# First chunk of a decaying-state attention kernel: the tables zeroed by ScalarE, the ones filled behind the power table, own-key columns from that table, and other due times

## The chip, the cores and the metric

The kernel runs on one core of a Trainium2 chip. The metric is the device time of one execution in microseconds (us), the median over several. Engines are named as the profile names them: PE (matmul, with PEld for its weight loads), DVE (VectorE), ACT (ScalarE), POOL (GpSimd), SP (SyncE, which here only issues transfers).

## The reference

Two parts follow one another. The first is attention with a state that decays, for 4 batches, 8 heads, 768 times and 48 channels; the second is an MLP on its output:

```
for t in range(S):
    cur = einsum('bhd,bhe->bhde', u[None] * k_t, v_t)
    y[:, :, t] = einsum('bhd,bhde->bhe', r_t, state + cur)
    state = w[None, :, :, None] * state + einsum('bhd,bhe->bhde', k_t, v_t)
x = y as [B*S, H*D] = [3072, 384]
out = gelu(x @ w_in) @ w_out          # w_in [384, 2048], w_out [2048, 384]
```

## The kernel before

**Chunks and groups.** The 768 times are cut into 6 chunks of 128; a chunk of all 4 batches is 512 columns for the MLP. The 8 heads go in pairs, so each chunk has 4 groups. Inside a chunk the recurrence is written as products: r and k of a group are scaled by powers of the decay w, their product gives the scores, past scores are kept by a mask, and the scores times v are the output. The own-time term (u) is a sum of r times k, weighted.

**The MLP.** A chunk takes 16 steps. Each has 9 products of 512 columns into `Hp` (L667: x times w_in, in high and low parts), gelu twice on ACT (`gh`, L696, and `gf`, L697), the low part on DVE (`gl`, L698), and 9 products into `O` (L709). The weights come in 64-bit words and are split into `wh` and `wl` during the first chunk, a weight pair for each step, by four ACT and three DVE operations (L382 to L395).

**The order.** Each operation is entered with `add(engine, ns, due, function, r=reads, w=writes)`. `Plan.run` walks a model of the engines with these assumed durations and issues what is ready, by due time; an operation that is entered with `LATER` takes its due time from those that need it. That fixes each engine's order. The names in `r` and `w` set only the planned order: waits on the chip come from the tiles that an instruction really reads and writes. Where the plan sees PE idle it fills in matmuls on zeros (`heat`, L283).

**The first chunk.** SP issues the loads one behind the other: `wu_sb` (w and u), then `T` and `N` of group 0, of group 1, and so on, with the first weights from the seventh on. Meanwhile:

- POOL fills `ones`, makes the masks `diag`, `past` and `ident` of it (L250), and zeroes `Fm` (L265) and `VO` (L266) twice each, `UB` (L330), `E` (L341) and `Am` (L268, twice).
- DVE zeroes `zeros` (the operand of `heat`), and makes the power table `F` from w: it limits w to its range (L303), doubles the powers (L297), and multiplies by a reciprocal. Then it makes `E1`, whose transpose gives `WN`.
- A group scales `T` by `F` (L555), multiplies its halves into `KB` (L559; POOL, for group 0 DVE), and has `N` scaled by `WN` on POOL (L561). PE makes the scores (L568, into `A` or `AE`) and the own sums (L573: `KB` times the columns of `UB`, into `UE`). DVE puts the past scores into `Fm` (L599) and the own sums times v into `VO` (L602). PE multiplies `VO` and `Fm` into `Y` (L588, L594); groups 1 to 3 first add columns of group 0 (`gaps`, L583). ACT and DVE take `Y` as the high and low part of x (L534, L535: `x3` for group 0, `xx` for the others). First sums for the state (L578) are copied to `Sa` (L612), which frees the PSUM banks that `Hp` and `O` take over.
- `UB` holds w times u for each pair: `uw` is made on DVE (L319, L320) and copied into place on POOL (L325).

Of the kernel before, what the change touches and what calls it, by code (L numbers as in the profile page):

```python
# [9 lines left out]
F32 = mybir.dt.float32  # L10
# [5 lines left out]
ALU = mybir.AluOpType  # L16
# [5 lines left out]
C = 128  # L22
# [3 lines left out]
NB = B  # L26
TOK = NB * C
NJ = DF // 128
HALF = 64
# [8 lines left out]
LATER = 10 ** 7  # L38
# [8 lines left out]
class Plan:  # L47
# [11 lines left out]
    def add(self, eng, ns, at, fn, r=(), w=()):  # L59
        n = len(self.ops)  # L60
        deps = set()
        for x in r:
            deps.add(self.writer.get(x))
            self.readers.setdefault(x, []).append(n)
        for x in w:
            deps.add(self.writer.get(x))
            deps.update(self.readers.pop(x, ()))
            self.writer[x] = n
        deps -= {None, n}
        self.ops.append((eng, ns, at, fn, deps))  # L70
        self.reads.append(set(r))
# [66 lines left out]
def rwkv_gelu_mlp(tc, rkT, rkv, wuT, uN, wmlp, r, k, vT, w, u, out):  # L138
    nc = tc.nc
    with ExitStack() as ctx:  # L140
# [21 lines left out]
        w_sb = wu_sb[:, 0:2 * NP]  # L162
        u_lane = wu_sb[:, 2 * NP:]
# [8 lines left out]
        E = sb([LP, NP, 2, HALF], F32, "E")  # L172
        F = sb([LP, NP, C], F32, "F", pro)
# [3 lines left out]
        UB = sb([LP, NP, 2], F32, "UB", pro)  # L177
        Fm = [sb([C, 2, NB, C], F32, f"Fm{i}", pro) for i in range(2)]
        VO = [sb([C, NB, 2, 64], F32, f"VO{i}", pro) for i in range(2)]
        uw = sb([LP, 2 * NP], F32, "uw")  # L180
# [4 lines left out]
        Am = [sb([C, 2, NB, HALF], F32, f"Am{i}") for i in range(2)]  # L185
# [11 lines left out]
        zeros = sb([128, 512], F32R, "zeros", pro)  # L197
# [4 lines left out]
        add, dma = plan.add, plan.dma  # L202
        dve = lambda n: 65 + n / 0.96
        dve2 = lambda n: 65 + n / 1.92
        act = lambda n: 95 + n / 1.2
        sdve = lambda n: 145 + n / 0.96
        sdve2 = lambda n: 145 + n / 1.92
        sact = lambda n: 250 + n / 1.2
        pool = lambda n: 110 + n * 2.15
# [35 lines left out]


        add("pool", 140, 0, lambda: nc.gpsimd.memset(ones, 1.0), w=["ones"])

        def masked(dst, base, cm, op):
            nc.gpsimd.affine_select(out=dst, in_=ones, pattern=[[1, C]], base=base, channel_multiplier=cm,  # L250
# [5 lines left out]
        for dst, src, x in ((diag2, diag, "diag"), (past2, past, "past")):  # L256
            for h in range(2):
                add("act", 280, LATER, lambda dst=dst, src=src, h=h: nc.scalar.copy(
                    out=dst[64 * h:64 * h + 64], in_=src[64 * h:64 * h + 64, 64 - 64 * h:128 - 64 * h]),
                    r=[x], w=[f"{x}2{h}"])  # L260
        add("dve", 80, -10 ** 6, lambda: nc.vector.memset(warm, 0.0), w=["warm"])
        add("act", 1400, -10 ** 6, lambda: nc.scalar.activation(out=warm, in_=warm, func=AF.Gelu), w=["warm"])
        add("dve", 480, -20, lambda: nc.vector.memset(zeros.bitcast(F32), 0.0), w=["zeros"])
        for i in range(2):
            add("pool", 1100, 10 + i, lambda i=i: nc.gpsimd.memset(Fm[i], 0.0), w=[f"Fm{i}"])  # L265
            add("pool", 560, 20 + i, lambda i=i: nc.gpsimd.memset(VO[i], 0.0), w=[f"VO{i}"])  # L266
        for i in range(2):
            add("pool", 560, LATER, lambda i=i: nc.gpsimd.memset(Am[i], 0.0), w=[f"Am{i}"])  # L268


        def spread_ones():
# [22 lines left out]
        one = lambda x, i: x[:, :, i:i + 1]  # L294
# [4 lines left out]
        by_half = lambda x: x.rearrange("l (p h) -> l p h", h=2)  # L299
# [22 lines left out]
        def own_columns():  # L322
            for x in range(2):
                l = slice(64 * x, 64 * x + D)
                nc.gpsimd.tensor_copy(out=UB[l, :, x:x + 1], in_=by_half(uw)[l, :, 0:1])  # L325

        add("dve", 2150, 5, powers, r=["w_sb"], w=["F"])
        add("dve", 800, LATER, state_powers, r=["F"], w=["E1"])
        add("dve", 330, LATER, own_weights, r=["w_sb"], w=["uw"])
        add("pool", 110, LATER, lambda: nc.gpsimd.memset(UB, 0.0), w=["UB"])  # L330
        add("pool", 300, LATER, own_columns, r=["uw"], w=["UB"])


        def flip():
# [3 lines left out]
        add("pe", 700, LATER, flip, r=["E1", "ident"], w=["O1"])  # L338
        add("act", 500, LATER, lambda: nc.scalar.copy(
            out=WN, in_=AE[:, 1].rearrange("s (p j x) -> s p j x", p=NP, x=64)[:, :, :, :D]), r=["O1"], w=["WN"])  # L340
        add("pool", 560, LATER, lambda: nc.gpsimd.memset(E, 0.0), w=["E0"])  # L341


        def for_halves():
# [201 lines left out]
        def first_group(gi):  # L546
            g = Group(gi)
            i = gi % 2
            at = lambda ns: 4000 + 4300 * gi + ns
# [2 lines left out]
            fm, FM = Fm[i], f"Fm{i}"  # L552
            vo, VN = VO[i], f"VO{i}"
            flat = g.t.rearrange("l a b t -> l (a b) t")
            add("dve", sdve(1024), at(0), lambda: nc.vector.tensor_tensor(  # L555
                out=flat, in0=flat, in1=F[:, g.p].unsqueeze(1).to_broadcast([LP, 2 * NB, C]), op=ALU.mult),
                r=["F"], w=[g.T])
            eng, ns = (nc.gpsimd, 1300) if gi else (nc.vector, sdve(512))
            add("pool" if gi else "dve", ns, at(100), lambda: eng.tensor_tensor(  # L559
                out=own, in0=g.t[:, 1], in1=g.t[:, 0, :, ::-1], op=ALU.mult), r=[g.T], w=OWN)  # L560
            add("pool", pool(DM), LATER, lambda: nc.gpsimd.tensor_tensor(  # L561
                out=g.kn, in0=g.kn, in1=WN[:, g.p].rearrange("s j d -> s (j d)").unsqueeze(1).to_broadcast(
                    [C, NB, 2 * D]), op=ALU.mult), r=["WN"], w=[g.K])
# [27 lines left out]
            def first_new():  # L591
# [8 lines left out]
                out=fm, mask=past.bitcast(U32).unsqueeze(1).unsqueeze(1).to_broadcast([C, 2, NB, C]),  # L600
                data=g.x.rearrange("s x (b t) -> s x b t", t=C)), r=["past"] + g.X, w=[FM])
            add("dve", sdve(DM), at(3300), lambda: nc.vector.tensor_tensor(  # L602
                out=vo[:, :, :, :D], in0=g.vn.rearrange("s b (j d) -> s b j d", d=D),
                in1=sums.rearrange("s (b j) -> s b j", j=2).unsqueeze(3).to_broadcast([C, NB, 2, D]), op=ALU.mult),
                r=[SU, g.V], w=[VN])
            if spreads(g):
# [6 lines left out]
                out=g.s[2].rearrange("l b e -> l (b e)"), in_=g.u[:LP, g.u0:g.u0 + NB * D]), r=g.U, w=g.S[2])  # L613
# [242 lines left out]
        for G in range(NSTEP + 1):  # L856
# [12 lines left out]
            if G % 4 == 0 and G // 4 + NP < NG:  # L869
                gi = G // 4 + NP + 1  # L870
# [110 lines left out]
```

## Time and profile before

| what | us |
|---|---|
| median of 3 runs | 495.92 (495.48 to 496.24) |
| the profiled execution, its own time | 494.16 |
| its span on the core | 492.7 |
| PE busy | 480.5 (98%) |
| DVE busy | 227.9 (46%) |
| ACT busy | 219.0 (44%) |
| POOL busy | 76.9 (16%) |

The shares are means over stages. In the first 37 us PE works in small products that wait for others; from then on it runs the MLP nearly without a gap. Times in the rows below are counted from the start of the span.

### The profile page before, as it was taken

How to read it: one execution, taken by the hardware profiler on the slowest of the kernel's cores; microseconds unless marked ns; L12 is line 12 of the kernel's file. 1: busy time of each engine (PE TensorE's matmuls, PEld its weight loads, DVE VectorE, ACT ScalarE, POOL GpSimd, SP SyncE). 2: the span in 40 equal slices, each digit the busy share in tenths (PEclk: the TensorE clock that was granted, in tenths of full speed). 3: DMA queues.
4: the chain of work that ended last, by engine and by line, in shares of the span. 5: the costliest groups of instructions: out<-in, count | busy, mean ns of one | idle time of the engine just before them, and what ended most of it. 6: DMA issues, size and time to landing. Idle time of an engine off the chain costs nothing.

```text
span 492.7 us, 10760 instructions
## 1 busy us (share of the span) xinstructions
PE 480.5 (98%) x4684; PEld 389.0 (79%) x4684; DVE 227.9 (46%) x348; ACT 219.0 (44%) x449; POOL 76.9 (16%) x79
## 2 busy tenths in 40 slices
PE   6989999999999999999999999999999999999996
PEld 5877877878888878788888888888888887888885
DVE  7678889895525426414435434344344132211112
ACT  2179999976343343523342542442533423322222
POOL 6620100113012023302022021021120200000000
PEclk8799999999999999999999999999999999999999
DMA  8943666721403304303203313123223000100001
GB/s 242 354 117 122 237 205 208 225 56 53 142 2 97 97 2 130 118 0 97 72 27 97 113 39 98 37 60 98 79 72 97 1 14 12 65 1 0 1 0 67
DMA packets 13331, 43.79 MB, mean 89 GB/s; under 512 B 1824, under 2 KB 2208, under 8 KB 13280
## 3 DMA queue, kind: packets, MB, share of 16 engines
q1 hardware_dynamic: 13280, 43.07, 27.9%
q8 instruction: 37, 0.61, 0.5%
q14 instruction: 14, 0.11, 0.1%
HBM read 36.38 MB, written 4.72 MB: 83 GB/s over the span
## 4 chain that ended last, share of the span: by engine, by line
PE 90%; ACT 4%; DVE 4%; POOL 1%; issue 0%; DMA 0%; DVEq 0%; POOLq 0%
PE Hp L667 39%; PE O L709 38%; PE Y L480 2%; PE A L460 2%; PE Y L500 2%; PE Y L709 1%; PE A L471 1%; ACT wb L386 1%; DVE T L555 1%; PE Y L588 1%; DVE F L303 1%; PE Y L594 1%; POOL N L561 1%; ACT wb L388 1%; ACT wh L394 1%; ACT gf L697 1%
## 5 line engine op out<-in xcount | busy, mean ns | idle before, releaser
L667 PE MATMUL Hp<-xx,wh 128*128 128x512 f32 x576 | 166.7, 397 | 1.9 <-ACT gf L697 1.2
L698 DVE TENSOR_TENSOR gl<-gf,gh 128x512 fp32r<-128x512 f32 x95 | 68.9, 725 | 191.2 <-ACT gf L697 191.0
L696 ACT ACTIVATE gh<-Hp 128x512 fp32r<-128x512 f32 x95 | 56.7, 597 | 215.6 <-PE Hp L667 215.6
L667 PEld LDWEIGHTS Hp<-xx,wh 128*128 128x128 f32 x576 | 106.5, 188 | 28.3 <-ACT gf L697 3.3
L667 PE MATMUL Hp<-xx,wl 128*128 128x512 f32 x288 | 83.7, 398 | 0.9 <-DVE wl L395 0.9
L709 PE MATMUL O<-gh,wh 128*128 128x512 f32 (+1 forms) x285 | 82.0, 394 | 0.0
L709 PE MATMUL O<-gl,wh 128*128 128x512 f32 (+1 forms) x285 | 80.6, 390 | 0.0
L709 PE MATMUL O<-gh,wl 128*128 128x512 f32 (+1 forms) x285 | 80.6, 390 | 0.0
L667 PEld LDWEIGHTS Hp<-xx,wl 128*128 128x128 f32 x288 | 53.9, 188 | 14.4 <-DVE wl L395 1.7
L709 PEld LDWEIGHTS O<-gh,wh 128*128 128x128 f32 x285 | 52.5, 188 | 12.6
L709 PEld LDWEIGHTS O<-gl,wh 128*128 128x128 f32 x285 | 52.6, 188 | 11.7
L709 PEld LDWEIGHTS O<-gh,wl 128*128 128x128 f32 x285 | 52.5, 188 | 11.5
L431 POOL TENSOR_TENSOR Nb<-Nb 128x384 f32<-128x384 f32 x16 | 19.6, 1226 | 250.1 <-DMA Nb<-in_rkv_dram 220.0
L697 ACT ACTIVATE gf<-Hp 128x512 f32<-128x512 f32 x96 | 56.9, 593 | 0.0
L451 ACT ACTIVATE Am<-diag,cs 128x64 f32<-128x64 f32 x128 | 33.6, 341 | 10.1 <-DVE cs L446 9.5
L433 POOL TENSOR_TENSOR Nb<-Nb,WN 128x384 f32<-128x384 f32 x20 | 24.1, 1208 | 47.0 <-DMA Nb<-in_rkv_dram 44.4
L427 DVE TENSOR_TENSOR Tb<-Tb,E 112x1024 f32<-112x1024 f32 x20 | 24.4, 1221 | 4.7 <-DMA Tb<-in_rkT_dram 4.5
L446 DVE TENSOR_REDUCE cs<-Nb 128x8 f32<-128x384 f32 x16 | 8.8, 553 | 34.4 <-POOL Nb L443 34.3
L386 ACT ACTIVATE wb<-raw 128x768 uint16<-128x768 uint32 (+1 forms) x17 | 17.6, 1036 | 0.0
L388 ACT ACTIVATE wb<-raw 128x768 f16<-128x768 f32 (+1 forms) x17 | 17.6, 1034 | 0.0
L392 DVE CUSTOM_DVE_ANT_0 wa<-wa,wb 128x1536 uint16<-128x1536 uint16 (+1 forms) x17 | 16.3, 957 | 2.5 <-ACT wb L388 2.1
L443 POOL TENSOR_TENSOR Nb<-Nb,u_sb 128x384 f32<-128x384 f32 x16 | 17.0, 1064 | 0.1
(126 smaller groups left out, 400.1 us busy)
## 6 DMA issues: line engine op xcount, KB each, us to landing
raw<-in_wmlp_dram SPq DMA_DIRECT2D x15, 768.0 KB, 4.3
Nb<-in_rkv_dram SPq DMA_DIRECT2D x16, 576.0 KB, 5.4
Tb<-in_rkT_dram SPq DMA_DIRECT2D x20, 448.0 KB, 4.3
out_dram<-raw SPq DMA_DIRECT2D x5, 768.0 KB, 3.6
xx<-x SPq DMA_DIRECT2D x30, 64.0 KB, 4.2
T<-in_rkT_dram SPq DMA_DIRECT2D x4, 448.0 KB, 6.9
N<-in_rkv_dram SPq DMA_DIRECT2D x4, 384.0 KB, 7.4
Nb<-in_rkv_dram SPq DMA_DIRECT2D x4, 384.0 KB, 8.4
```

What stands on the lines that cost most here:

```text
L386: add("act", sact(n), LATER, lambda: nc.scalar.activation(out=parts[:, :, 0], in_=lo.bitcast(U32), func=AF.Copy, scale=2.0 ** -29), r=R_, ...
L388: add("act", sact(n), LATER, lambda: nc.scalar.activation(out=parts[:, :, 1].bitcast(F16), in_=hi.bitcast(F32), func=AF.Copy, scale=2.0 ** ...
L427: add("dve", sdve(1024), LATER, lambda: nc.vector.tensor_tensor(out=flat, in0=flat, in1=E[:, g.p].rearrange("l h i -> l (h i)").unsqueeze( ...
L431: add("pool", pool(DM), LATER, lambda: nc.gpsimd.tensor_tensor(out=g.n[:, 0], in0=g.n[:, 0], in1=g.n[:, 1], op=ALU.mult), r=[g.K], w=[g.R])
L433: add("pool", pool(DM), LATER, lambda: nc.gpsimd.tensor_tensor(out=g.kn, in0=g.kn, in1=WN[:, g.p].rearrange("s j d -> s (j d)").unsqueeze( ...
L443: add("pool", pool(DM), LATER, lambda: nc.gpsimd.tensor_tensor(out=g.n[:, 0], in0=g.n[:, 0], in1=u_sb[:, g.p, :].unsqueeze(1).to_broadcast ...
L451: add("act", sact(HALF) + 60, LATER, lambda x=x, b=b: nc.scalar.activation(out=g.am[:, x, b, :], in_=diag2, func=AF.Copy, scale=g.sums[:, ...
L667: nc.tensor.matmul(O[3], lhsT=wt[j][:, 0, k_ * 128:(k_ + 1) * 128], rhs=x[:, a, k_, :], start=start and k_ == ks[0], stop=stop and k_ == k ...
L696: add("act", 600, LATER, lambda: nc.scalar.activation(out=high, in_=O[3], func=AF.Gelu), r=["H"], w=[GH])
L697: add("act", 600, LATER, lambda: nc.scalar.activation(out=gf, in_=O[3], func=AF.Gelu), r=["H"], w=["gf"])
L698: add("dve", sdve(512), LATER, lambda: nc.vector.tensor_tensor(out=low, in0=gf, in1=high.bitcast(F32), op=ALU.subtract), r=["gf", GH], w=[GL])
L709: nc.tensor.matmul(bank(dst)[:, a:b], lhsT=wt[j][:, 1, d * 128:(d + 1) * 128], rhs=gt[:, a:b], start=(j == 0 and n == 0), stop=(j == NJ - ...
```

## The change

ScalarE zeroes `Fm` and `VO` by copying from `zeros`; the zeroing of `E` and `Am` is entered with `r=["F"]`; `UB` is computed by DVE from the table and u in place of the copies from `uw`; the plan is told 2900 ns for the table where it was told 2150; and scaling `T` of groups 1 to 3 is due 2500 ns sooner. Behind these edits the planner puts all engines' work of the first chunk in a new order.

```diff
         add("pool", 140, 0, lambda: nc.gpsimd.memset(ones, 1.0), w=["ones"])
+        add("dve", 480, -20, lambda: nc.vector.memset(zeros.bitcast(F32), 0.0), w=["zeros"])
...
-        add("dve", 480, -20, lambda: nc.vector.memset(zeros.bitcast(F32), 0.0), w=["zeros"])
         for i in range(2):
-            add("pool", 1100, 10 + i, lambda i=i: nc.gpsimd.memset(Fm[i], 0.0), w=[f"Fm{i}"])
-            add("pool", 560, 20 + i, lambda i=i: nc.gpsimd.memset(VO[i], 0.0), w=[f"VO{i}"])
-        for i in range(2):
-            add("pool", 560, LATER, lambda i=i: nc.gpsimd.memset(Am[i], 0.0), w=[f"Am{i}"])
+            add("act", 560, 20 + i, lambda i=i: nc.scalar.copy(
+                out=VO[i].rearrange("s b j d -> s (b j d)"), in_=zeros.bitcast(F32)), r=["zeros"], w=[f"VO{i}"])
+            add("act", 1050, 10 + i, lambda i=i: nc.scalar.copy(
+                out=Fm[i].rearrange("s j b t -> s j (b t)"),
+                in_=zeros.bitcast(F32).unsqueeze(1).to_broadcast([C, 2, NB * C])), r=["zeros"], w=[f"Fm{i}"])
...
-                nc.gpsimd.tensor_copy(out=UB[l, :, x:x + 1], in_=by_half(uw)[l, :, 0:1])
-
-        add("dve", 2150, 5, powers, r=["w_sb"], w=["F"])
+                nc.vector.tensor_tensor(out=UB[l, :, x:x + 1], in0=one(F, HALF + 1)[l], in1=by_half(u_lane)[l, :, 0:1],
+                                        op=ALU.mult)
+
+        add("dve", 2900, 5, powers, r=["w_sb"], w=["F"])
+        for i in range(2):
+            add("pool", 560, LATER, lambda i=i: nc.gpsimd.memset(Am[i], 0.0), r=["F"], w=[f"Am{i}"])
...
-        add("pool", 110, LATER, lambda: nc.gpsimd.memset(UB, 0.0), w=["UB"])
-        add("pool", 300, LATER, own_columns, r=["uw"], w=["UB"])
+        add("pool", 110, -1, lambda: nc.gpsimd.memset(UB, 0.0), w=["UB"])
+        add("dve", 350, 200, own_columns, r=["F", "w_sb"], w=["UB"])
...
-        add("pool", 560, LATER, lambda: nc.gpsimd.memset(E, 0.0), w=["E0"])
+        add("pool", 560, LATER, lambda: nc.gpsimd.memset(E, 0.0), r=["F"], w=["E0"])
...
-            add("dve", sdve(1024), at(0), lambda: nc.vector.tensor_tensor(
+            add("dve", sdve(1024), at(-2500 * (gi > 0)), lambda: nc.vector.tensor_tensor(
```

In the orders below, the numbers behind a name tell buffers apart: `T_110` to `T_113` are groups 0 to 3 and `N_118` to `N_121` likewise; `KB_116`, `VO_106`, `Fm_104` serve groups 0 and 2, `KB_117`, `VO_107`, `Fm_105` groups 1 and 3. Line numbers of the changed kernel are 1 to 4 higher.

POOL at the start, with the waits that its instructions carry; before:

```order
L247 MEMSET ones 128x128
L265 MEMSET Fm_104 128x1024
...
L250 AFFINE_SELECT ident<-ones 128x128
L265 MEMSET Fm_105 128x1024
L266 MEMSET VO_106 128x512
L266 MEMSET VO_107 128x512
L330 MEMSET UB 112x8
L341 MEMSET E 112x512
L268 MEMSET Am_124 128x512
L345 COPY E<-F 112x4x64 [waits DVE_49,Pool_49]
```

and changed:

```order
L247 MEMSET ones 128x128
L334 MEMSET UB 112x8
...
L251 AFFINE_SELECT ident<-ones 128x128
L345 MEMSET E 112x512
L331 MEMSET Am_124 128x512
L349 COPY E<-F 112x4x64 [waits DVE_49,Pool_49]
```

Four zeroings are gone from this row; those of `E` and the first `Am` still stand directly behind the masks, and neither carries a wait.

PE from the last `heat` of the warm-up to the outputs of group 0; before:

```order
L283 MATMUL UE<-zeros 128x512 x5
L568 MATMUL A<-T_110 128x128 x8
L283 MATMUL UE<-zeros 128x512 x2
L573 MATMUL UE<-UB,KB_116 128x2 x4
L336 MATMUL AE<-ident,E_100 128x112 x4
L283 MATMUL UE<-zeros 128x512
L588 MATMUL Y<-diag,VO_106 112x128 x4
L594 MATMUL Y<-Fm_104,N_118 48x128 x8
L568 MATMUL AE<-T_111 128x128 x8
L573 MATMUL UE<-UB,KB_117 128x2 x4
```

and changed, up to the first `gaps`:

```order
L284 MATMUL UE<-zeros 128x512 x8
L572 MATMUL A<-T_110 128x128 x8
L577 MATMUL UE<-UB,KB_116 128x2 x4
L284 MATMUL UE<-zeros 128x512 x4
L340 MATMUL AE<-ident,E_100 128x112 x4
L577 MATMUL UE<-UB,KB_117 128x2 x4
L592 MATMUL Y<-diag,VO_106 112x128 x4
L572 MATMUL AE<-T_111 128x128 x8
L598 MATMUL Y<-Fm_104,N_118 48x128 x8
L572 MATMUL A<-T_112 128x128 x8
L577 MATMUL UE<-UB,KB_116 128x2 x4
L572 MATMUL AE<-T_113 128x128 x8
```

Own sums of group 1 and scores of group 1 moved in front of the outputs of group 0, and the scores of group 3 in front of the first `gaps`; there are 12 heats in place of 8 here.

ACT ahead of the first gelu; before:

```order
L394 CAST wh_75<-wa_139 128x384
L534 CAST xx_128<-Y 128x512
L612 COPY Sa<-UE 112x192 x2
L382 ACTIVATE wa_141<-raw_138 128x768
L386 ACTIVATE wb_142<-raw_138 128x768
L394 CAST wh_76<-wa_140 128x768
L696 ACTIVATE gh_131<-Hp 128x512
```

and changed:

```order
L538 CAST xx_128<-Y 128x512
L616 COPY Sa<-UE 112x192
L398 CAST wh_76<-wa_140 128x768
L616 COPY Sa<-UE 112x192 x2
L386 ACTIVATE wa_141<-raw_138 128x768
L390 ACTIVATE wb_142<-raw_138 128x768
L392 ACTIVATE wb_142<-raw_138 128x768
L700 ACTIVATE gh_131<-Hp 128x512
```

The last two copies to `Sa` moved behind a cast of 768 columns.

## Rows read from the trace of the kernel before

**Rows 1.** The page's costliest groups: busy, mean ns, idle before and releaser.

```profile
L667 PE MATMUL Hp<-xx,wh 128*128 128x512 f32 x576 | 166.7, 397 | 1.9 <-ACT gf L697 1.2
...
L667 PE MATMUL Hp<-xx,wl 128*128 128x512 f32 x288 | 83.7, 398 | 0.9 <-DVE wl L395 0.9
```

**Rows 2.** Windows of PE: stretch in us, busy, instructions, PEclk, DMA share, GB/s.

```profile
8.00:9.00 1.00, 0.00 (x0) 1.00 1.05 356
9.00:10.00 1.00, 0.74 (x6) 0.55 1.02 272
...
19.00:20.00 1.00, 1.00 (x16) 0.83 1.05 290
```

**Rows 3.** Timeline of the start (start us, us, ...); the last row: line 761's group.

```profile
1.18 0.96 POOL L265 MEMSET Fm<- 128x1024 f32 x1
...
2.65 0.29 POOL L250 TENSOR_SCALAR_AFFINE_SELECT ident<-ones 128x128 f32<-128x128 f32 x1
2.66 3.10 DVE L303 TENSOR_SCALAR F<-wu_sb 112x4 f32<-112x4 f32 x1 [0.91 <-DMA wu_sb<-in_wuT_dram]
...
5.21 0.52 POOL L268 MEMSET Am<- 128x512 f32 x1
...
L761 DVE TENSOR_SCALAR low<-wu_sb x1: 165/165/165, 152.7 to 152.7; 112x8 f32<-112x8 f32 x1
```

**Rows 4.** SP's loads of T for groups 0 and 1; each with its landing, us from issue.

```profile
1.51 0.41 SPq L231 DMA_DIRECT2D T<-in_rkT_dram  x1
T<-in_rkT_dram SPq DMA_DIRECT2D x1, 448.0 KB, 4.2
...
2.43 0.43 SPq L231 DMA_DIRECT2D T<-in_rkT_dram  x1
T<-in_rkT_dram SPq DMA_DIRECT2D x1, 448.0 KB, 6.1
```

**Rows 5.** Timeline, DVE and POOL in groups 0 and 1.

```profile
7.98 1.22 DVE L555 TENSOR_TENSOR T<-T,F 112x1024 f32<-112x1024 f32 x1
...
10.85 0.69 DVE L297 TENSOR_TENSOR E<-F,P 112x512 f32<-112x512 f32 x1
...
14.08 0.56 DVE L602 TENSOR_TENSOR VO<-N,UE 128x384 f32<-128x384 f32 x1 [1.33 <-PE UE L573]
...
16.58 2.25 POOL L559 TENSOR_TENSOR KB<-T 112x512 f32<-112x512 f32 x1
...
19.75 1.26 POOL L559 TENSOR_TENSOR KB<-T 112x512 f32<-112x512 f32 x1
```

**Rows 6.** Timeline, PE: the same products at the two clocks, and own sums.

```profile
9.26 2.08 PE L568 MATMUL A<-T 48*128 48x128 f32 x16 [2.43 <-DVE T L555]
...
15.28 1.91 PE L588 MATMUL Y<-diag,VO 128*112 128x128 f32 x8
...
20.23 1.05 PE L573 MATMUL UE<-UB,KB 112*128 112x2 f32 x8
...
21.22 1.16 PE L568 MATMUL A<-T 48*128 48x128 f32 x16
...
23.59 1.13 PE L588 MATMUL Y<-diag,VO 128*112 128x128 f32 x8
```

**Rows 7.** Timeline from the first cast to the MLP; the AE row: chain that ended last.

```profile
19.11 0.58 ACT L534 CAST x<-Y 112x512 fp32r<-112x512 f32 x1 [3.76 <-PE Y L594]
...
22.98 0.56 DVE L602 TENSOR_TENSOR VO<-N,UE 128x384 f32<-128x384 f32 x1 [0.68 <-POOL N L561]
...
27.87 1.09 PE AE L568 x16
...
36.33 0.54 ACT L612 COPY Sa<-UE 112x192 f32<-112x192 f32 x2
...
36.93 0.50 PE L667 MATMUL Hp<-xx,wh 128*128 128x512 f32 x1 [0.64 <-ACT Sa L612]
...
38.51 0.83 ACT L394 CAST wh<-wa 128x768 fp32r<-128x768 f32 x1
```

## The prediction

> **What bounds the kernel now.** I read the page first: PE is busy in 98% of the span, and in all 864 products into `Hp` it stood idle for 2.8 us [rows 1]. From the first of them at 36.93 on, what PE does is fixed; only the moment at which that stretch begins can move. So I went to the windows of PE's first 24 us, the timeline up to 40 us and the chain of waits. The windows hold a surprise: the granted clock is 1.00 while PE waits idle at 8 to 9 us, then 0.50 (the level of 1.2 GHz instead of 2.4) from 9.1 until 19.34, where the window from 19 to 20 still has a mean of 0.83 [rows 2]. The fall came after an idle stretch. The same 16 score products took 2.08 us at the low level and 1.16 at the full one, the 8 of `Y<-diag,VO` 1.91 and 1.13 [rows 6]. **A product at the low level thus loses 0.41 to 0.44 of its time**; I take 0.43.
>
> The timeline shows the wait that the change is about. DVE's limiting of w, 4 columns, starts at 2.66 and takes 3.10 us; the same kind of operation on 8 columns takes 0.165 us at 152.7 us, where POOL has nothing to do. It ends at 5.76, 0.03 behind the last zeroing in POOL's row of memsets, which began its 0.52 us at 5.21 [rows 3].
>
> **Step by step, all products first at the full clock.**
>
> *The table.* 3.10 becomes 0.165 if POOL is silent, so `F` would be there 2.9 us sooner. It isn't silent at once. Before, the `ident` select ended at 2.94 with an `Fm` zeroing of 0.96 ahead of it [rows 3]; now only the tiny `UB` zeroing is ahead, so it ends near 2.1. Then `E` and `Am` follow without a wait, 0.52 each, to about 3.1. The limiting is held from 2.66 to 3.1: `F` comes some 2.6 us sooner, near 5.3, and the two new `UB` products (0.16 each, as the short operation in [rows 3]) make it 5.6. The bounds are 5.0 with no hold and 6.2 if the row ends only at 4.0. `T` of group 0 lands at 1.51 + 4.2 = 5.7 [rows 4], so scaling starts at 5.8 in place of 7.98 [rows 5], and the uncertainty above costs 0 to 0.5. `spread` now stands ahead of the table on DVE and needs `ident` (2.1); w lands only at 2.6, so that is hidden.
>
> *ScalarE's zeroing.* A cast of 768 columns on ACT takes 0.83 [rows 7], so the two copies of 1024 and two of 512 are about 3.3 us. They need only `zeros` and stand at the start, where ACT's next work waits for the powers, and `Fm` isn't touched before 11 us. Cost nothing; with 1 us more still nothing.
>
> *Outputs of group 0.* This is what the new order ties together: own sums of group 1 must be done before `Y<-diag,VO_106`. `T` of group 1 lands at 2.43 + 6.1 = 8.5 [rows 4], is scaled until 9.8 and multiplied into `KB_117` by POOL: 1.26 alone, 2.25 where it ran beside a DVE multiply [rows 5]. Its neighbour on DVE is now `E1`, 0.69 us. If `KB_117` goes first it ends at 11.1 and `E1` at 11.6; the transposes (about 0.5, half of the eight of `Y<-diag` at full clock [rows 6]) stand ahead of the sums on PE, so these run from 12.1 to 13.15 [rows 6]. If `E1` goes first, the sums end at 12.8. I take the longer way; the other is 0.35 better. The Trainium skill (SBUF — State Buffer, Who interferes with whom) says that a DVE instruction with two SBUF inputs and a GpSimd instruction that reads SBUF exclude each other, and that the one issued first has the ports for its whole length. By that rule the longer way is right and the sum stays as it is; the row of 2.25 alone, in which POOL gave way, would have made it 0.35 less.
>
> `VO` 0.56 more makes 13.75, then PE has `Y<-diag` 1.1, scores of group 1 1.1, `Y<-Fm` 1.0: the first cast at 17.1 instead of 19.11 [rows 7]. **−2.0 us.**
>
> *Groups 1 to 3.* Group 3 is scaled before, not behind, the outputs of group 1, so its scores (1.09 on the chain at 27.87) leave the chain; and `VO_107` no longer waits 0.68 for POOL's scaled `N` [rows 7]. **−1.8 us.** The bounds are −0.7 (one of them only) and −2.5.
>
> *Entry into the MLP.* `Hp` waits for the last copies to `Sa`, 0.64 us at the end [rows 7]. Behind the change a cast of 0.83 us [rows 7] stands in front of them on ACT, and PE, `Hp` and both gelus are queued behind: **+0.8 us**, at best +0.3 if the last sums come late anyway.
>
> *Later.* `uw` moves behind all this, to where its first reader comes; the weight loads are freed by splits that run earlier, so the fourth is issued sooner and lands behind the same queue. PE waited only 0.9 us for a split weight before [rows 1], and the splits move at least as far as PE does: nothing.
>
> Sum at the full clock: −2.0 − 1.8 + 0.8 = **−3.0 us**.
>
> **The clock.** Now the part that the rows do not settle. The idle stretch before 9.1 goes: more heats and then the scores fill PE up to 8.7. But a thin one takes its place: between 8.7 and 13.8 PE has 4 heats, 4 transposes and own sums, which are mostly weight loads, and it waits for `KB_117` and `VO_106`. I expect the clock to fall in or just behind it. Before, it came back at 19.34 [rows 2], 4.1 us after the dense products into `Y` had begun at 15.28 [rows 6]. If it does likewise, 4.1 us from 13.8 on are at the low level, and 4.1 × 0.43 = 1.8 us are lost. **Forecast: −3.0 + 1.8 = −1.2 us.** The Trainium skill (TensorE: Matmul & The Clock Gate, Part 1) says that the moment at which the clock changes moves by some half microsecond from run to run; no run here shows more than one execution's clock.
>
> **The rivals.**
> 1. *The clock never falls.* For it: PE has no idle gap as long as the one before 9.1. Against it: little is multiplied for 5 us. −3.0 us: 492.9.
> 2. *It falls and stays low for 6.8 us from 13.8 on*, since the scores and the last `Y<-Fm` use part of the array and dense work is broken by casts. 6.8 × 0.43 = 2.9: 495.8, no change to be measured.
> 3. *Slower:* it stays low for 10.2 us as before, now over the products of groups 0 to 2, all of which hold the chain, where part of the old low stretch lay beside waits. 10.2 × 0.43 = 4.4, so +1.4: 497.3. The turning point is 7 us at the low level.
> 4. *The holding back does nothing:* `E` and `Am` are zeroed at once, as the order shows. This is in the sum; without the landing of `T` at 5.7 behind it, it would cost 0.4.
>
> **How the numbers follow.** The profiled execution took 494.16, its span 492.7 and 1.5 around it; the median of the runs, 495.92, lies 1.8 above. The sum of −1.2 makes 493.0 of that execution and 494.7 of the median, which I predict. Chances: forecast 0.32, rival 1 0.20, rival 2 0.30, rival 3 0.18; rival 4 is no case of its own. 0.2% is 1.0 us, about what a measurement can tell from no change. Rival 1 and three quarters of the forecast are faster: 0.44. The rest of the forecast and nine tenths of rival 2 are the same: 0.35. Rival 3 and the rest of rival 2 are slower: 0.21. The range leaves out half of each end, 492.9 to 497.0; the forecast's own, with the bounds of its terms, is 493.9 to 495.5.
>
> **What would show it.** Right: limiting w ends near 3.3 us, scaling of group 0 starts at 5.7 to 5.9 behind a landing, group 1's at 8.5, the sums from `KB_117` end near 13, and the windows show 0.50 for about 4 us somewhere between 12 and 19. The first cast is near 18.5 and the first `Hp` near 35.7, with ACT's cast of `wh` in front of the last `Sa`. Wrong: limiting w still takes over 1 us; the clock at 1.00 throughout, or at 0.50 for 7 us or more; or PE waiting for `wl` after 60 us, which would give back what the start gained.

## The result, and the profile of the changed kernel

The changed kernel is **slower**: a median of 498.79 us (494.65 to 501.94, 19 runs) against 495.48 (492.73 to 496.63, 19 runs) for the kernel before, ratio 1.0066 with an interval of [1.0046, 1.0085]. Beside the experiments it was run again: 497.06 against 495.32, ratio 1.0034 [1.0011, 1.0056]. The forecast of 494.7 had the wrong sign, and the median lies above the range. The ratios and intervals, here and in the table below, leave out runs that took over 1.5% more than the fastest of their kernel: one of e13 and three of e14.

The profiled execution took 495.69 us, with a span of 494.2. Each run also comes with its span and its mean granted clock, and (1 − clock) × 2 × span is the time that it spent at the low level (0.50). In the changed kernel that time goes from 7.9 to 23.0 us, 14.9 in the middle of 31 runs, and a straight line through these runs is

time = 490.8 us + 0.45 × (microseconds at the low clock), correlation 0.95.

The clock of a run is given to three decimals, so each of these times is known to about half a microsecond. A part of them costs nothing, because it lies at the end, where no product runs any more: 2.3 us in the profile before, 0.7 in that of the changed kernel. One of these windows before (stretch in us, busy, instructions, granted clock, DMA share, GB/s):

```profile
491.00:492.00 1.00, 0.00 (x0) 0.50 0.00 0
```

The kernel before had 6.9 to 15.9 such microseconds, 9.9 in the middle of 115 runs. Five more of them at 0.45 are 2.2 us, about the difference between the two kernels (497.4 in the middle of the 31 runs, 495.3 in that of the 115). The runs of the kernel before follow a flatter line of their own less closely (0.29 for each, correlation 0.58), so this is an estimate. The first thing to look at is therefore the clock, and what stood ahead of it.

Windows of PE in the changed kernel, with the same columns, to be laid beside [rows 2]:

```profile
10.00:11.00 1.00, 0.72 (x4) 1.00 1.10 276
11.00:12.00 1.00, 0.00 (x0) 1.00 0.97 274
12.00:13.00 1.00, 0.64 (x4) 0.61 1.03 290
...
18.00:19.00 1.00, 1.00 (x14) 0.50 1.05 401
19.00:20.00 1.00, 1.00 (x18) 0.98 0.98 274
...
31.00:32.00 1.00, 0.69 (x4) 1.00 0.06 25
32.00:33.00 1.00, 0.96 (x18) 0.85 0.06 16
...
35.00:36.00 1.00, 1.00 (x14) 0.50 1.01 418
36.00:37.00 1.00, 1.00 (x36) 0.94 0.11 45
```

There are **two** low stretches, 12.2 to 19.0 and 32.7 to 36.1, where the kernel before had one. Each begins behind a place where PE waited: the window from 11 to 12 is empty, and in that from 31 to 32 it is busy for 0.69.

The timeline shows the steps of the change (start us, us, engine, line, operation, and in brackets the idle time before and what ended it):

```profile
2.51 0.53 POOL L331 MEMSET Am<- 128x512 f32 x1
2.78 0.28 DVE L304 TENSOR_SCALAR F<-wu_sb 112x4 f32<-112x4 f32 x1 [0.26 <-DMA wu_sb<-in_wuT_dram]
...
4.32 1.13 ACT L265 COPY VO<-zeros 128x512 f32<-128x512 f32 x2
...
6.28 1.23 DVE L559 TENSOR_TENSOR T<-T,F 112x1024 f32<-112x1024 f32 x1 [0.80 <-DMA T<-in_rkT_dram]
...
9.08 1.23 DVE L559 TENSOR_TENSOR T<-T,F 112x1024 f32<-112x1024 f32 x1 [0.85 <-DMA T<-in_rkT_dram]
...
10.40 1.27 POOL L563 TENSOR_TENSOR KB<-T 112x512 f32<-112x512 f32 x1 [4.02 <-DVE P L298]
10.42 1.79 DVE L298 TENSOR_TENSOR E<-F,P 112x512 f32<-112x512 f32 x1
...
12.36 0.98 PE L340 MATMUL AE<-ident,E 112*128 112x112 f32 x4 [1.63 <-DVE E L298]
...
13.13 1.73 PE L577 MATMUL UE<-UB,KB 112*128 112x2 f32 x8
...
15.56 2.05 PE L592 MATMUL Y<-diag,VO 128*112 128x128 f32 x8 [0.70 <-DVE VO L606]
...
20.46 0.59 ACT L538 CAST x<-Y 112x512 fp32r<-112x512 f32 x1 [6.61 <-PE Y L598]
...
27.70 0.59 ACT L538 CAST xx<-Y 128x512 fp32r<-128x512 f32 x1 [3.64 <-PE Y L592]
28.34 1.08 PE L598 MATMUL Y<-Fm,N 128*48 128x128 f32 x16 [0.68 <-ACT xx L538]
...
39.08 0.50 PE L671 MATMUL Hp<-xx,wh 128*128 128x512 f32 x1 [0.64 <-ACT Sa L616]
```

Limiting w takes 0.28 us in place of 3.10 [rows 3], and the scaling of group 0 begins at 6.28 in place of 7.98 [rows 5]. That lead is gone by `Y<-diag,VO`: 15.56 against 15.28 [rows 6]. **Between them stands `E1`.** On DVE it now comes behind the scaling of group 1, which waited for its load until 9.08. Then it meets POOL's `KB` of group 1, issued 0.02 us ahead of it, and takes 1.79 us, 0.53 beyond the end of `KB`. The transposes wait for it, idle for 1.63 us on PE, the own sums of group 1 stand behind the transposes, and the outputs of group 0 behind those. There the clock falls, and transposes, own sums and `Y<-diag` take 0.98, 1.73 and 2.05. The first cast comes at 20.46 (before: 19.11 [rows 7]), the first `Hp` at 39.08 (before: 36.93). Of these 2.15 us the MLP gives 0.65 back by its twelfth step, and the span is 1.5 longer.

The page says the same of the MLP as before: its products into `Hp` stood idle for 1.9 + 0.9 us.

```profile
L671 PE MATMUL Hp<-xx,wh 128*128 128x512 f32 x576 | 166.5, 397 | 1.9 <-ACT gf L701 1.2
...
L671 PE MATMUL Hp<-xx,wl 128*128 128x512 f32 x288 | 83.5, 397 | 0.9 <-DVE wl L399 0.9
```

### The profile page after: what moved, and what is told of

It reads as the page before. It is cut to its first block, busy times and chain, and to the rows that moved or that the text cites. A ratio compares the mean times of both kernels' runs of the same rounds, so it can differ in the third digit from the quotient of the medians.

```text
span 494.2 us, 10774 instructions
## 1 busy us (share of the span) xinstructions
PE 480.8 (97%) x4689; PEld 390.2 (79%) x4689; DVE 228.1 (46%) x350; ACT 221.8 (45%) x453; POOL 72.1 (15%) x73
## 4 chain that ended last, share of the span: by engine, by line
PE 92%; ACT 3%; DVE 2%; DMA 1%; issue 1%; SPq 0%; DVEq 0%
PE Hp L671 39%; PE O L713 39%; PE Y L484 2%; PE A L464 2%; PE Y L504 2%; DMA T<-in_rkT_dram 1%; PE Y L592 1%; PE Y L713 1%; PE A L475 1%; PE Y L598 1%; ACT wb L390 1%; PE AE L572 1%; ACT wb L392 1%; PE UE L582 0%; DVE E L298 0%
## 5 line engine op out<-in xcount | busy, mean ns | idle before, releaser
L671 PEld LDWEIGHTS Hp<-xx,wl 128*128 128x128 f32 x288 | 53.9, 188 | 14.3 <-DVE wl L399 1.5
L437 POOL TENSOR_TENSOR Nb<-Nb,WN 128x384 f32<-128x384 f32 x20 | 25.1, 1259 | 50.4 <-DMA Nb<-in_rkv_dram 39.7
L431 DVE TENSOR_TENSOR Tb<-Tb,E 112x1024 f32<-112x1024 f32 x20 | 25.4, 1270 | 6.7 <-DMA Tb<-in_rkT_dram 6.6
L538 ACT CAST xx<-Y 112x512 fp32r<-112x512 f32 (+1 forms) x18 | 10.6, 588 | 18.9 <-PE Y L504 11.4
```

Of the source, the lines that this page charges most:

```text
L431: add("dve", sdve(1024), LATER, lambda: nc.vector.tensor_tensor(out=flat, in0=flat, in1=E[:, g.p].rearrange("l h i -> l (h i)").unsqueeze( ...
L671: nc.tensor.matmul(O[3], lhsT=wt[j][:, 0, k_ * 128:(k_ + 1) * 128], rhs=x[:, a, k_, :], start=start and k_ == ks[0], stop=stop and k_ == k ...
```

## The experiments

Two theories were put against each other. **Clock**: what costs time is PE's thin stretches, because the low clock follows them. **Order**: the waits in the new order cost time by themselves, whatever the clock. In the table the medians stand beside the kernel before on the same chip, and the last column is the time at the low clock in the middle run.

| run | median us | ratio to before, interval | low clock us |
|---|---|---|---|
| changed kernel | 498.79 | 1.0066 [1.0046, 1.0085] | 17.9 |
| changed kernel, again (e8) | 497.06 | 1.0034 [1.0011, 1.0056] | 14.4 |
| e1: due times as before | 493.35 | 0.9953 [0.9928, 0.9978] | 6.4 |
| e2: plan told 2150 ns | 492.82 | 0.9928 [0.9898, 0.9959] | 2.9 |
| e12: the same again | 493.56 | 0.9956 [0.9935, 0.9977] | 4.9 |
| e11: both | 492.79 | 0.9958 [0.9934, 0.9981] | 4.9 |
| e3: before, zeroing moved | 493.41 | 0.9944 [0.9918, 0.9970] | 5.9 |
| e4: before, due sooner | 496.67 | 1.0050 [1.0017, 1.0084] | 12.4 |
| e5: changed, 8 more heats | 493.85 | 0.9973 [0.9954, 0.9991] | 4.9 |
| e6: changed, 13 more heats | 493.88 | 0.9986 [0.9964, 1.0008] | 1.0 |
| e13: changed, 5 more heats | 494.16 | 0.9973 [0.9947, 0.9998] | 4.9 |
| e7: 2150 ns, fewer heats | 495.26 | 0.9999 [0.9976, 1.0022] | 11.8 |
| e10: 2150 ns, 4 more heats | 492.37 | 0.9933 [0.9909, 0.9957] | 3.5 |
| e9: before, 9 more heats | 493.97 | 0.9971 [0.9950, 0.9992] | 6.9 |
| e14: changed, `E1` ahead | 491.09 | 0.9906 [0.9880, 0.9931] | 2.5 |

Each row has 12 runs, but the first 19, e2 7, e3 and e10 8. The kernel before had a median of 495.1 to 495.5 and 9.9 to 10.9 us at the low clock in these sessions.

### Which part of the change loses: e1, e2, e11, e3, e4

**e1**, the changed kernel with the due times of the scaling as before:

```diff
-            add("dve", sdve(1024), at(-2500 * (gi > 0)), lambda: nc.vector.tensor_tensor(
+            add("dve", sdve(1024), at(0), lambda: nc.vector.tensor_tensor(
```

> The changed kernel with the scaling of groups 1 to 3 due as before (the 2500 ns taken back); the rest of the change stays. Theory 'order': the sooner due times put own sums and scores of group 1 ahead of the outputs of group 0, the scores of group 3 ahead of the first gaps, and the cast of group 1 behind a product of group 2; without them the first products into Hp start 1 to 2 us sooner at an equal clock, and a fit of time against the microseconds at the low granted clock (0.48 us each in the changed kernel, constant 490.4) has a constant 1 to 2 us lower. Theory 'clock': the order costs nothing, only the microseconds at the low clock do; the constant stays within 0.5 us of 490.4 and the median moves by 0.48 us per microsecond at the low clock.

**e2**, the changed kernel with the plan's duration of the table as before:

```diff
-        add("dve", 2900, 5, powers, r=["w_sb"], w=["F"])
+        add("dve", 2150, 5, powers, r=["w_sb"], w=["F"])
```

> The changed kernel with the plan told 2150 ns for the table, as before; the sooner due times stay. The order then has the scores of group 1 ahead of its own sums, 5 heats in the thin stretch where there were 4, and the casts of groups 1 and 2 further apart. Theory 'order': the constant of the fit falls by 1 to 2 us, since PE waits less before the outputs of group 0. Theory 'clock': the constant stays at 490.4, and the median goes down only if the thin stretch filled better keeps the clock up (less than 18 us at the low level in the middle run).

**e11**, both edits together:

> The changed kernel with both of its edits to the plan's numbers undone (table told 2150 ns, due times as before): zeroing by ScalarE, zeroing of E and Am entered behind the table, and own columns from the table remain. Theory 'the plan's numbers made the loss': 492.5 to 494, 1.5 to 3 us faster than before, with 3 to 7 us at the low clock. Rival 'own columns from the table cost': near 495 or above, since the kernel before with the zeroing alone moved had 493.4.

**e3**, the kernel before with the zeroing alone:

```diff
-            add("pool", 1100, 10 + i, lambda i=i: nc.gpsimd.memset(Fm[i], 0.0), w=[f"Fm{i}"])
-            add("pool", 560, 20 + i, lambda i=i: nc.gpsimd.memset(VO[i], 0.0), w=[f"VO{i}"])
-        for i in range(2):
-            add("pool", 560, LATER, lambda i=i: nc.gpsimd.memset(Am[i], 0.0), w=[f"Am{i}"])
+            add("act", 560, 20 + i, lambda i=i: nc.scalar.copy(
+                out=VO[i].rearrange("s b j d -> s (b j d)"), in_=zeros.bitcast(F32)), r=["zeros"], w=[f"VO{i}"])
+            add("act", 1050, 10 + i, lambda i=i: nc.scalar.copy(
+                out=Fm[i].rearrange("s j b t -> s j (b t)"),
+                in_=zeros.bitcast(F32).unsqueeze(1).to_broadcast([C, 2, NB * C])), r=["zeros"], w=[f"Fm{i}"])
...
+        for i in range(2):
+            add("pool", 560, LATER, lambda i=i: nc.gpsimd.memset(Am[i], 0.0), r=["F"], w=[f"Am{i}"])
...
-        add("pool", 560, LATER, lambda: nc.gpsimd.memset(E, 0.0), w=["E0"])
+        add("pool", 560, LATER, lambda: nc.gpsimd.memset(E, 0.0), r=["F"], w=["E0"])
```

> The kernel before with the zeroing of Fm and VO alone given to ScalarE, and E and Am entered behind the table; own columns, table length and due times as before. Theory 'the zeroing is worth what it should be': limiting w takes under 0.4 us, the table is 2.5 us sooner, and at an equal clock the kernel is 1.5 to 2.5 us faster than before. Rival: what comes sooner waits for its loads or meets the low clock, and the median is within 0.5 us of before or above it, with more microseconds at the low clock than before.

**e4**, the kernel before with the sooner due times alone:

```diff
-            add("dve", sdve(1024), at(0), lambda: nc.vector.tensor_tensor(
+            add("dve", sdve(1024), at(-2500 * (gi > 0)), lambda: nc.vector.tensor_tensor(
```

> The kernel before with the scaling of groups 1 to 3 due 2500 ns sooner and nothing else. Theory 'order': the outputs of group 0 are tied to group 1's scaling here too; slower than before by 1 to 2 us at an equal clock. Theory 'clock': PE's idle stretch at 7 to 9 us is the same as before, the low stretch begins at the same place, and the time is that of before within 0.5 us.

Measured: e1 493.35, e2 492.82, e11 492.79, e3 493.41, e4 496.67. **The zeroing gains 1.7 us, and the plan's two numbers together lose it and more**: either of them taken back (e1, e2) makes the changed kernel 3.5 to 6 us faster, as fast as with both taken back (e11), and the sooner due times alone make the kernel before slower. The own columns cost nothing that shows (e11 against e3). In all five the time at the low clock moves with the median. e1 and e3 at 6.9 to 7.9 us of it take 493.2 to 495.6, the kernel before at as many 493.4 to 495.3, so at an equal clock the constant did not fall as the theory "order" had it. Nor is e3 faster by 1.5 to 2.5 us at an equal clock, as was expected of it: its 1.7 us stand beside 4 us less at the low clock. e4 speaks for the theory "order" in part: five of its runs with 9.9 to 10.9 us at the low clock took 496.2 to 497.3, middle 496.6, the kernel before at as many 494.7 to 497.4, middle 496.0. In e4 the clock does not fall where it did before, though PE's idle stretch, 6.41 to 9.26, is even longer than the 6.84 to 9.26 before; windows of PE:

```profile
9.00:10.00 1.00, 0.74 (x12) 1.00 1.04 219
11.00:12.00 1.00, 0.44 (x3) 0.79 0.96 205
...
20.00:21.00 1.00, 1.00 (x14) 0.50 1.03 212
21.00:22.00 1.00, 1.00 (x10) 0.59 1.05 239
```

So the theory "clock" was wrong about this place: here the fall came at 11.6, 2.3 us behind the end of the idle stretch, and the clock stayed low as long as before (10.2 us).

### Is it the clock: e5, e6, e7, e8

**e5** adds products on zeros (heats) to the changed kernel where PE stood idle; it takes no work away. **e6** adds 5 more at the later places.

```diff
             def own_sums():
                 for b in range(NB):
                     nc.tensor.matmul(sums[:, 2 * b:2 * b + 2], lhsT=own[:, b, :], rhs=UB[:, g.p], start=True, stop=True)
+                for _ in range({0: 6, 1: 2}.get(gi, 0)):
+                    heat(UE[:, 1])
```

> The changed kernel with 8 more products on zeros, put where PE stood idle in its profile: 6 behind the own sums of group 0 (idle from 10.7 to 12.36) and 2 behind those of group 1 (14.86 to 15.56). They add work to PE and take none away. Theory 'clock': the first low stretch (12.2 to 19.0 in the profile) goes or shrinks, the time at the low granted clock falls from 17.9 us in the middle run to some 5 to 11, and the median falls by 0.48 us for each, 3 to 6 us in all, to 493 to 496. Theory 'order' (the waits themselves make the time, the clock is a companion): the same or up to 1 us slower than the changed kernel's 498.8.

> As the one with 8 more products on zeros, with 5 more in the later idle places of the changed kernel's profile: 3 behind the own-time product of group 2 (27.67 to 28.34) and 2 behind the own sums of group 3 (30.40 to 30.90). Theory 'clock': the second low stretch (32.7 to 36.05) goes too; the time at the low clock is below 6 us and the median 492 to 494, below before. Theory 'order': no faster than the changed kernel.

**e7** takes the planner's heats out of the kernel of e2:

```diff
-HEATS, HEAT_NS, HEAT_ROOM = 9, 320, 150
+HEATS, HEAT_NS, HEAT_ROOM = 9, 320, 10 ** 6
```

> The changed kernel told 2150 ns for the table, and without the products on zeros that the planner fills in (11 of them in the first chunk); the 9 of the first warm-up stay. Nothing that others wait for is added. Theory 'clock': the clock falls again, 8 us or more at the low level in the middle run, where the same kernel with them had 2.9, and it is 2 to 5 us slower than that one's 492.8. Theory 'order': 0 to 1 us faster than that one, since PE has less to do and waits for the same.

**e8** is the changed kernel unaltered.

> The changed kernel itself once more, beside the others and with a second profile. All theories: 497 to 500, 14 to 20 us at the low clock in the middle run. What the profile may tell: where the low stretches lie in another execution; by theory 'clock' they begin at or just behind PE's idle places at 10.7 to 12.4 and 30.4 to 32, and the number of them, not their place, makes the time.

**More work for PE made the kernel 3 to 5 us faster.** e5 has 493.85 with 4.9 us at the low clock, and its profile has none in the first chunk (windows of PE):

```profile
10.00:11.00 1.00, 1.00 (x8) 1.00 0.98 259
11.00:12.00 1.00, 1.00 (x7) 1.00 1.09 330
12.00:13.00 1.00, 1.00 (x8) 1.00 1.02 259
...
31.00:32.00 1.00, 1.00 (x14) 1.00 0.50 66
```

The theory "order" expected the same or slower and falls as the explanation of the loss. e6 lowers the low time to 1.0 us but gains nothing over e5. With at most 2.0 us at the low clock its runs took 492.6 to 494.1, those of e5 492.2 to 493.2; that its heats cost what they save is likely and not shown. e7 has 11.8 us at the low clock and 495.26, as expected; but five of its 12 runs took 495.4 to 497.8 with only 0 to 4.0 us recorded as low, which the recorded clock does not explain, so e7 is weak evidence. e8's profile shows the two low stretches in another place, 13.4 to 20.3 and 30.5 to 37.3 (windows of PE):

```profile
13.00:14.00 1.00, 0.30 (x2) 0.72 1.05 367
...
20.00:21.00 1.00, 1.00 (x16) 0.87 1.00 384
...
30.00:31.00 1.00, 0.50 (x1) 0.75 0.00 0
...
37.00:38.00 1.00, 0.64 (x20) 0.83 0.00 0
```

### What the sooner table is worth: e9, e10, e12

**e9** leaves the kernel before as it is and fills its idle stretch:

```diff
             for n in range(HEATS):
                 heat([x[:, i] for x in (UE, YU, AA, AE) for i in range(2)][n % 8])
+            for n in range(9):
+                heat(UE[:, 1])
```

> The kernel before, its long zeroing row and late table kept, with 9 more products on zeros behind the first five, where PE stood idle from 6.84 to 9.26. Theory 'clock alone': its low stretch from 9.1 to 19.34 goes or is short (middle run below 5 us at the low clock), and the median falls by 2 to 3 us to 492.5 to 493.5, as fast as the best order of the changed kernel, so that the sooner table is worth nothing by itself. Rival 'the sooner table is worth 2 us at full clock': the low stretch goes all the same, but the median stays at 494 or above, 1.5 us or more behind the changed kernel told 2150 ns.

**e10** adds 4 heats to the kernel of e2: two at the end of the gaps of group 2, two behind the own sums of group 3.

```diff
+                for _ in range({3: 2}.get(gi, 0)):
+                    heat(UE[:, 1])
...
+                for _ in range(2 * (gi == 2)):
+                    heat(UE[:, 1])
```

> The changed kernel told 2150 ns for the table, with 4 more products on zeros at two idle places of its profile: 2 ahead of the own-time product of group 2 (22.7 to 23.4) and 2 behind the own sums of group 3 (26.5 to 27.05). Theory 'clock': the time at the low clock, 2.9 us in the middle run without them, goes to 0 to 1, and the median falls by up to 1 us to about 492. Rival: the four products only delay, and it is 0 to 1 us slower than without them.

**e12** is the kernel of e2 unaltered.

> The changed kernel told 2150 ns for the table once more, for a second profile. It had 492.8 and in its profile the clock at 1.00 throughout, but lost 2.1 us near 190 us, where one load of Nb took 6.5 us to land against 4.3 in the kernel before. If that is fixed by the order, the load takes over 6 us again; if it is chance, it differs. 492 to 493.5 either way.

e9 has 493.97, 1.4 us faster than before: the clock still fell, but later and for less (11.9 to 18.7 in its profile; windows of PE):

```profile
11.00:12.00 1.00, 0.45 (x4) 0.94 1.02 331
...
18.00:19.00 1.00, 1.00 (x12) 0.65 1.07 358
```

Neither forecast of e9 was met as it stands: the low time stayed at 6.9 us, and the median lies 0.4 to 1.2 us behind e12 and e2. Its three runs with at most 2.0 us at the low clock took 492.4 to 493.3; the six such runs of e2 and e12 took 490.4 to 492.9, with a middle of 491.2, and the three of e1 491.9 to 492.3. So **at full clock the sooner table seems to be worth 1 to 2 us** when the order lets it through. This is not settled: few runs say it, the heats of e9 may hold something back themselves, and at 6.9 to 7.9 us of low time e1 and e3 showed no gain. e10 has 492.37, within the scatter of e2 and e12; its low time did not go down to 0 to 1 us (3.5).

e2 and e12 are one program, and both profiles have the full clock throughout the first chunk, yet their spans are 491.3 and 489.2. All of it lies near 190 us, behind transfers issued from 182.5 us on. The first of them among the DMA issues of e2 (size and us from issue to landing):

```profile
Nb<-in_rkv_dram SPq DMA_DIRECT2D x1, 576.0 KB, 6.5
```

PE behind it in the timeline of e2:

```profile
190.63 0.47 PE L671 MATMUL Hp<-xx,wh 128*128 128x512 f32 x1 [0.55 <-DMA xx<-x]
...
193.21 0.57 PE L475 MATMUL A<-Nb 64*48 64x48 f32 x32 [1.04 <-POOL Nb L437]
```

And the same load in e12:

```profile
Nb<-in_rkv_dram SPq DMA_DIRECT2D x1, 576.0 KB, 4.1
```

Landing after 6.5 us it held POOL, and POOL held PE for 1.04; PE had already waited 0.55 for the transfer of `xx` that was issued behind it. In e12 neither wait is there. In 6 of the 16 profiles this load took 6.1 to 6.6 us, in the others 4.1 to 5.7. A chance of up to 2 us of this kind can lie in any run, and is one reason why single executions say little about edits of this size.

### By which wait: e13, e14

**e13** puts 3 heats behind the own sums of group 0 and 2 ahead of its own-time product:

```diff
+                for _ in range({0: 3}.get(gi, 0)):
+                    heat(UE[:, 1])
...
             def own_new():
+                for _ in range(2 * (gi == 0)):
+                    heat(UE[:, 1])
```

> The changed kernel with 5 more products on zeros, placed so that nothing waits behind them: 3 behind the own sums of group 0 and 2 ahead of the own-time product of group 0, which waits for VO there. Theory 'the changed order costs 1 to 2 us at full clock as well': runs with under 2.5 us at the low clock take 492 to 493, as with 8 more products, and the first product into Hp comes at 35 or later where the clock did not fall. Rival 'the order is free, the 8 heats were in the way': such runs take 490.5 to 491.5, as the order with 2150 ns, with the first product into Hp near 34.

**e14** changes one number of the changed kernel, the due time of `E1`:

```diff
-        add("dve", 800, LATER, state_powers, r=["F"], w=["E1"])
+        add("dve", 800, 300, state_powers, r=["F"], w=["E1"])
```

> The changed kernel with one more number of the plan changed: the products that make E1 are due at 300 instead of by their users, which puts them on DVE ahead of the scaling of group 0, so that no landing of a load of T stands ahead of them. Both numbers of the change (2900 ns, 2500 ns sooner) stay. Theory 'E1 behind group 1's T is the wait': E1 takes 0.7 us near 6, the transposes no longer come at 12.4, PE's idle stretch from 10.7 to 12.3 and with it the first low stretch go, VO of group 0 is there by 12, and the median is 491 to 493, some 5 us below the changed kernel. Rival 'any order with the scaling 2500 ns sooner loses': 495 or above, with 10 us or more at the low clock.

e13's three runs with at most 2.0 us at the low clock took 492.1 to 492.6, those of e5 (five) 492.2 to 493.2. So at full clock the changed order is no better than the kernel before (e9: 492.4 to 493.3), and 1 to 2 us behind the order told 2150 ns. The first `Hp` of the profiles without a low stretch says as much: 35.56 (e5) and 34.80 (e6) against 34.07 (e2) and 33.94 (e12); e13's own profile has a low stretch of 3.4 us and can't tell. How much of that is the heats is not settled: in e13 too, two of them waited for `VO` and held `Y<-diag` for 0.57 us. e14's timeline:

```profile
5.82 0.69 DVE L298 TENSOR_TENSOR E<-F,P 112x512 f32<-112x512 f32 x1
...
7.57 0.55 PE L340 MATMUL AE<-ident,E 112*128 112x112 f32 x4
...
12.70 0.55 DVE L606 TENSOR_TENSOR VO<-N,UE 128x384 f32<-128x384 f32 x1 [0.68 <-issue]
...
32.23 0.50 PE L671 MATMUL Hp<-xx,wh 128*128 128x512 f32 x1 [0.55 <-ACT Sa L616]
```

and its windows of PE where the first low stretch of the changed kernel lay:

```profile
12.00:13.00 1.00, 0.59 (x18) 1.00 1.00 263
13.00:14.00 1.00, 0.65 (x17) 1.00 1.02 278
```

**`E1` ahead of the loads takes 0.69 us, the transposes come at 7.57 in place of 12.36, and the first `Hp` at 32.23 in place of 39.08.** With both of the plan's numbers kept, the median of all 12 runs is 491.09, ratio 0.9906 [0.9880, 0.9931] to the kernel before: faster than both kernels. The rival, that any order with the sooner scaling loses, falls for the median. But three of the 12 runs had 13.8, 20.9 and 24.9 us at the low clock and took 495.8, 498.6 and 500.0: with `E1` ahead a long time at the low clock is rarer, not gone. `VO` came at 12.70 and not by 12. The edit moved other work as well (scores of group 1 and first sums into the place of the waits, `N` of groups 0 and 1 ahead of `KB` on POOL), so how much of its 6 to 8 us over the changed kernel is that one wait is not shown.

## Why the prediction was wrong, point by point

- **The table: right.** Forecast: limiting ends near 3.1 to 3.3, `F` near 5.3. Measured: it starts at 2.78, ends at 3.06, 0.02 behind `Am`'s zeroing, and `F` is there at 5.24. ScalarE's zeroing took 3.1 us (forecast 3.3) and ended at 5.45, with nothing waiting for it. Group 0 is scaled from 6.28, 0.5 later than forecast, because its load landed that much later.
- **Outputs of group 0: the right chain, too cheap.** The own sums of group 1 did tie them to group 1's `T` and `KB`, and the longer way, with `E1` behind `KB`, was the one taken. It was longer than I had it: `E1` ended at 12.21, not 11.6. The Trainium skill (SBUF — State Buffer, Who interferes with whom) says that whoever issues first has the shared ports for the whole instruction. The rows agree: `KB`, 0.02 us ahead, kept its 1.27, and `E1` took 1.79 instead of 0.69. In the kernel before it was DVE's multiply, at 16.38, that came ahead of POOL's `KB` of 2.25 at 16.58, so that row was the same rule and no sign that POOL gives way to a DVE multiply that comes later. At full clock the first cast came at 18.56 (e5) or 18.10 (e13), where the sum had 17.1: 0.6 to 1.0 sooner than before in place of 2.0. Of that, two heats of e13 took 0.57; in e5 `VO` came 0.10 behind two others, so by estimate they took as much. DVE's multiply in the kernel before:

```profile
16.38 1.32 DVE L555 TENSOR_TENSOR T<-T,F 112x1024 f32<-112x1024 f32 x1
```

- **Groups 1 to 3: right at full clock.** From the first cast to the last it took 16.51 us before and 14.3 in e5, −2.2 against −1.8 forecast. In the profile of the changed kernel it took 15.9, with the second low stretch in it. What I had not seen is the cast of group 1: it came at 27.70, 1.6 us behind its last product, since in the new order it stands behind the own-time product of group 2, and PE then waited 0.68 for it.
- **Entry into the MLP: another wait than the one forecast.** From the last cast to the first `Hp`: 1.31 before, 2.72 now, so +1.4 where the sum had +0.8 for a cast of `wh` ahead of the last copies to `Sa`. That cast did go ahead, but it ended at 38.13, and ACT then stood idle for 0.35: the copies waited for the last of the first sums on PE. These came behind an earlier copy to `Sa`, for which PE waited 0.42, and behind one of the planner's heats, which started 0.42 ahead of them:

```profile
37.08 0.32 ACT L616 COPY Sa<-UE 112x192 f32<-112x192 f32 x1
37.29 0.84 ACT L398 CAST wh<-wa 128x768 fp32r<-128x768 f32 x1
37.45 0.49 PE L284 MATMUL UE<-zeros 128*128 128x512 f32 x1 [0.42 <-ACT Sa L616]
37.87 0.56 PE L582 MATMUL UE<-N 128*48 128x48 f32 x16
...
38.48 0.54 ACT L616 COPY Sa<-UE 112x192 f32<-112x192 f32 x2 [0.35 <-PE UE L582]
```

- **The sum at full clock: −3.0 forecast.** e5's profile, with the full clock as long as products run, has its first `Hp` 1.4 sooner than the profiled execution before (−0.6 − 2.2 + 1.4) and a span of 490.7, −2.0. Part of that is not the change: the sum set products at full clock against a kernel before that ran 10.2 us at the low one. The kernel before itself, in the three runs of e9 at nearly full clock, took 492.4 to 493.3, as little as e5 and e13 (heats are added in all three). So against a kernel before at full clock this order gained close to nothing.
- **The clock: the step that failed.** "I expect the clock to fall in or just behind it. ... If it does likewise, 4.1 us from 13.8 on are at the low level, and 4.1 × 0.43 = 1.8 us are lost." It fell behind the thin stretch, at 12.2, and each microsecond cost 0.45. But it stayed down for 6.8 us, and **fell a second time** at 32.7, behind the waits of groups 2 and 3, of which the prediction has no word. In the middle run the low time was 14.9 us, end included, which at 0.45 is 6.7 us where the sum had 1.8. I had taken a single execution's return (4.1 us behind the first dense products) as a length that carries over.
- **Rival 3 came nearest**, and I gave it 0.18. It had 10.2 us at the low level and +1.4; the profiled execution had 10.2 us and +1.5. That is luck in part: the rival had one stretch, over groups 0 to 2, where the profile has two, the second over the outputs of group 3. Rival 2's 6.8 us is the length of the first stretch in both profiles of the changed kernel; the reason given for it no run tests. The median lies higher still than rival 3, because the profiled execution is at the lower end of the changed kernel's runs. The Trainium skill (TensorE: Matmul & The Clock Gate, Part 1) gives half a microsecond to either side for the moment at which the clock rises in sustained products. The products here are not sustained, and this case does not agree: in the two profiles of this one program each rise lies 1.2 us apart, the first fall 1.2 and the second 2.2. The runs differ by 15 us in their low time, so half a microsecond is no measure of the scatter here.

## What to carry to other kernels

Where a first stage is made of small products, ask of each new place where PE waits not only how long it waits but what the clock does behind it: here 8 idle-filling products were worth 3 to 5 us, and a table made 2.7 us sooner at most some 2. A planner's due time that is set sooner moves work that waits for a load ahead of work that is ready; in an engine's fixed order, put what is ready and needed by all (`E1`) ahead of what waits for a landing. And measure an edit of half a per cent on many runs, with each run's clock beside its time, since one profile can lie anywhere within them.

## What the runs showed of the hardware that had not been expected

- One program spends very different times at the low clock: 7.9 to 23.0 us in the changed kernel, and its time goes with it from 494.65 to 501.94 us, 0.45 for each.
- A load of 576 KB landed after 4.1 us or after 6.5 us in two executions of one program; with the transfers behind it, it moved the end by 2.1 us.
- A limiting of 4 columns on DVE lasts as long as POOL's whole row of zeroings and not only the one under way: 3.10 us with six of them still to come [rows 3], 0.28 beside the last one.
- The granted clock of the first microseconds reads 1.00 while products still run slowly. In e13's profile two products on zeros take 1.05 us from 4.51 on, eight of them 2.69 from 5.36, where two of the same take 0.73 from 14.34 on:

```profile
4.51 1.05 PE L284 MATMUL AE<-zeros 128*128 128x512 f32 x2
5.36 2.69 PE L284 MATMUL UE<-zeros 128*128 128x512 f32 x8
...
14.34 0.73 PE L284 MATMUL UE<-zeros 128*128 128x512 f32 x2 [0.70 <-DVE VO L612]
```
